# Batch 0's scores with tokens on partitions, w_spatial split in one piece, phi's reductions in one step, and new orders

## The chip, the cores and the metric

The kernel runs on one core of a Trainium2 chip. Its engines run instruction streams of their own: TensorE (PE; its weight loads are PEld), VectorE (DVE), ScalarE (ACT), GpSimd (POOL), and SyncE (SP), which here issues every DMA. The metric is the device time of one execution in microseconds (us). The kernel before takes 427.18 us, the median of three runs from 427.04 to 427.68.

## The reference

Eight batches, eight heads, 576 tokens, head size 64, 32 memories, all in fp32 (w_in and w_out arrive as float64).

```python
a = exp(phi - max(phi, axis=2)); a = a / (sum(a, axis=2) + 1e-9)   # over the 576 tokens
k_m = einsum('bhsm,bhsd->bhmd', a, k); v_m = einsum('bhsm,bhsd->bhmd', a, v)
attn = softmax(q @ k_m.T / 8)                                      # over the 32 memories
x = (attn @ v_m).transpose(0, 2, 1, 3).reshape(B, 576, 512)
h = relu(x @ w_in); u, v = h[..., :512], h[..., 512:]
v_n = (v - mean(v)) / sqrt(var(v) + 1e-6)
v_s = einsum('ts,bsd->btd', w_spatial, v_n) + b_spatial[None, :, None]
out = (u * v_s) @ w_out
```

## The kernel before

Each fp32 factor of a large product is split in a hi and a lo part, and three products of them (hi·hi, hi·lo, lo·hi) are summed in PSUM. The lo part is x − hi; it comes either from a subtraction on VectorE, or from a matmul of hi with `minus` (the negative identity), which adds −hi to x in PSUM, and a copy on ScalarE. `ON_VECTOR` names the steps that VectorE takes; the others fall to ScalarE and GpSimd, or to TensorE for a lo part.

The attention is never formed. `products` multiplies the 32 memories of each head with w_in (`mp`, split to `mh`, `ml`), and `gate` and `units` multiply the softmaxed scores (`ah`, `al`) with that. `pu` is a tile of the units (`u`), `pv` a tile of the gated branch v, which is normalised (`rs` and `sh` on GpSimd, `vr` on ScalarE) and split to `vh`, `vl`; its last 64 tokens go to `t1`, `t2`. `ps` is the product with w_spatial's transpose (`wth`, `wtl`; the last 64 tokens and the bias in `ws1`, `ws2`), `g` = u·ps is split to `gh`, `gl`, and `po` is the product with w_out (`woh`, `wol`), copied to `o` and sent out.

Each function is a generator; its yields cut it into steps, and a step is a letter with an index: P memory_weights (phi, its maximum by two transposes `mt` and `mb`, its exponentials and their sum `es`), K memories (k and v, `kvm`, the sum over tokens into the spare columns of `kvm` by a matmul with `ones`, `den`, and the transposes `tk`, `tv` that become `kT`, `vT`), Q queries (`qT`), S scores (`sc`, `sm`, then `ah`, `al`), M products, V gate, U units, G spatial, O project; and for the weights D load_win, E and L decode_win (columns 512 to 1023, which `gate` uses, and 0 to 511, which `units` uses), X prepare_out, W load_spatial, T transpose_spatial (with a `minus` matmul for the lo parts, `wt`), B prepare_bias. The decode turns float64 words to fp32 by shifts and masks (L187, L193), joins (L210, L218) and a product (L223 on VectorE, L226 on GpSimd).

A dash after a letter is one batch ahead. `START` is the order of the steps of batch 0 with all weights and the beginning of batch 1; `PLAN` is the order that every later batch repeats. Each engine executes its instructions in this written order, so an instruction that waits holds everything behind it on its engine, DMA issues on SP too. PSUM gives four single banks (`ps1`: mt, mb, kvm, tk, tv, tq, sc, mp, pv, po) and two double ones (`ps2`: wt, pu, ps), taken in turn; the first use of a bank waits for the last reader of its tile before.

## Time and profile before

| | before |
|---|---|
| median of three runs | 427.18 us (427.04 to 427.68) |
| the profiled execution: its own time, its span | 425.99 us, 424.2 us |
| PE busy in the span | 393.2 us (93%) |
| DVE, ACT, POOL busy | 299.8, 236.0, 78.9 us |
| first `pu` matmul (L663) starts | 49.23 us |
| last `po` matmul (L741) starts | 419.24 us |

The span runs from the first to the last event that the profile records; the execution's own time is 1.8 us longer. A matmul's start is exact to the record, its end is modelled, so in a row of back-to-back matmuls the distance of starts is the cost.

### The profile page before, as it was taken

How to read it: one execution, taken by the hardware profiler on the slowest of the kernel's cores; microseconds unless marked ns; L12 is line 12 of the kernel's file. 1: busy time of each engine (PE TensorE's matmuls, PEld its weight loads, DVE VectorE, ACT ScalarE, POOL GpSimd, SP SyncE). 2: the span in 40 equal slices, each digit the busy share in tenths (PEclk: the TensorE clock that was granted, in tenths of full speed). 3: DMA queues.
4: the chain of work that ended last, by engine and by line, in shares of the span. 5: the costliest groups of instructions: out<-in, count | busy, mean ns of one | idle time of the engine just before them, and what ended most of it. 6: DMA issues, size and time to landing. Idle time of an engine off the chain costs nothing.

```text
span 424.2 us, 9280 instructions
## 1 busy us (share of the span) xinstructions
PE 393.2 (93%) x3828; PEld 331.6 (78%) x3828; DVE 299.8 (71%) x560; ACT 236.0 (56%) x446; POOL 78.9 (19%) x154
## 2 busy tenths in 40 slices
PE   0295998999999999999999999999999999999995
PEld 0172786968988897978888897979798888889884
DVE  1899998995999458955897568946996568834420
ACT  1677787737753376346743575436734476248321
POOL 1345056621200022022200121002100120003100
PEclk9999899999999999999999999999999999999999
DMA  7989935507840948073922659063914500020003
GB/s 287 377 320 289 169 133 181 87 26 132 216 122 16 162 161 181 2 90 109 215 79 55 126 171 168 1 131 109 195 59 69 113 2 2 2 99 2 0 26 99
DMA packets 85790, 50.69 MB, mean 119 GB/s; under 512 B 66226, under 2 KB 70322, under 8 KB 85748
## 3 DMA queue, kind: packets, MB, share of 16 engines
q1 hardware_dynamic: 85748, 50.10, 47.9%
q8 instruction: 30, 0.49, 0.5%
q14 instruction: 12, 0.10, 0.1%
HBM read 40.65 MB, written 9.44 MB: 118 GB/s over the span
## 4 chain that ended last, share of the span: by engine, by line
PE 75%; DVE 13%; DMA 5%; ACT 4%; issue 1%; POOL 1%; SPq 0%; POOLq 0%; DVEq 0%; ACTq 0%
PE ps L701 24%; PE po L741 20%; PE pu L663 11%; PE pv L597 9%; DMA raw<-in_moe_w_in_dram 4%; PE kvm L375 4%; PE mp L565 3%; PE sc L492 2%; DVE power L210 1%; DVE win_sb L218 1%; DVE gl L725 1%; DMA out_dram<-o 1%; DVE st L621 1%; DVE sm L512 1%; PE pv L607 1%
## 5 line engine op out<-in xcount | busy, mean ns | idle before, releaser
L701 PE MATMUL ps<-wth,vh 128*128 128x288 f32 x256 | 57.0, 304 | 0.7 <-ACT u L672 0.4
L626 POOL TENSOR_SCALAR rs<-mv 128x1 f32<-128x1 f32 (+1 forms) x40 | 9.6, 241 | 249.8 <-DVE mv L623 247.2
L723 ACT CAST gh<-g 128x512 fp32r<-128x512 f32 x32 | 19.8, 620 | 63.8 <-DVE g L712 63.8
L701 PE MATMUL ps<-wth,vl 128*128 128x288 f32 x256 | 55.0, 296 | 0.0
L701 PE MATMUL ps<-wtl,vh 128*128 128x288 f32 x256 | 54.5, 294 | 0.0
L741 PE MATMUL po<-woh,gl 128*128 128x512 f32 x128 | 50.9, 398 | 0.8 <-DVE gl L725 0.8
L741 PE MATMUL po<-woh,gh 128*128 128x512 f32 x128 | 50.5, 395 | 0.0
L701 PEld LDWEIGHTS ps<-wth,vh 128*128 128x128 f32 x256 | 41.0, 188 | 12.1 <-ACT mh L574 5.0
L741 PE MATMUL po<-wol,gh 128*128 128x512 f32 x128 | 50.3, 393 | 0.0
L747 ACT COPY o<-po 128x512 f32<-128x512 f32 x36 | 20.9, 586 | 44.1 <-PE po L741 27.5
L701 PEld LDWEIGHTS ps<-wth,vl 128*128 128x128 f32 x256 | 41.0, 188 | 0.3 <-DVE vl L641 0.3
L701 PEld LDWEIGHTS ps<-wtl,vh 128*128 128x128 f32 x256 | 41.0, 188 | 0.0
L636 ACT ACTIVATE vr<-vr,sh,rs 128x512 f32<-128x512 f32 (+1 forms) x40 | 32.6, 814 | 10.2 <-POOL sh L631 9.9
L621 DVE BATCH_NORM_STATS2 st<-vr 128x6 f32<-128x512 f32 (+1 forms) x40 | 27.4, 686 | 12.1 <-ACT vr L602 11.6
L712 DVE TENSOR_TENSOR g<-u,ps 128x576 f32<-128x576 f32 x32 | 23.4, 751 | 12.5 <-PE ps L701 12.5
L741 PEld LDWEIGHTS po<-woh,gl 128*128 128x128 f32 x128 | 24.0, 188 | 8.2 <-DVE gl L725 2.8
L544 DVE TENSOR_TENSOR al<-aT,ah 128x576 fp32r<-128x576 f32 x16 | 12.1, 754 | 24.5 <-ACT ah L542 24.5
L663 PE MATMUL pu<-ah,mh 128*128 128x288 f32 x128 | 28.6, 305 | 0.0
L741 PEld LDWEIGHTS po<-wol,gh 128*128 128x128 f32 x128 | 24.0, 188 | 4.8
L741 PEld LDWEIGHTS po<-woh,gh 128*128 128x128 f32 x128 | 24.1, 188 | 4.6
L663 PE MATMUL pu<-ah,ml 128*128 128x288 f32 x128 | 27.3, 294 | 0.0
L663 PE MATMUL pu<-al,mh 128*128 128x288 f32 x128 | 27.2, 293 | 0.0
(158 smaller groups left out, 893.2 us busy)
## 6 DMA issues: line engine op xcount, KB each, us to landing
kv_sb<-in_k_dram SPq DMA_DIRECT2D x8, 1152.0 KB, 8.1
kv_sb<-in_v_dram SPq DMA_DIRECT2D x8, 1152.0 KB, 9.6
out_dram<-o SPq DMA_DIRECT2D x32, 256.0 KB, 2.4
q_sb<-in_q_dram SPq DMA_DIRECT2D x28, 288.0 KB, 6.2
phi_sb<-in_phi_dram SPq DMA_DIRECT2D x8, 576.0 KB, 4.0
raw<-in_moe_w_in_dram SPq DMA_DIRECT2D x8, 512.0 KB, 7.9
raw_out<-in_moe_w_out_dram SPq DMA_DIRECT2D x4, 512.0 KB, 5.4
w_sb<-in_moe_w_spatial_dram SPq DMA_DIRECT2D x1, 1152.0 KB, 10.8
```

What stands on the lines that cost most here:

```text
L375: nc.tensor.matmul(kvm[r][32 * j : 32 * j + 32], phi_sb[halves[r], j, i, :], kv_sb[halves[r], j, :, i * D : (i + 1) * D], start=(i == 0), ...
L544: nc.vector.tensor_tensor(al[:, r], aT[:, r], ah[:, r, 0:S].bitcast(F32), op=ALU.subtract)
L565: nc.tensor.matmul(mps[r][32 * j : 32 * j + 32, :], vT[D * r : D * r + D, 32 * j : 32 * j + 32], win_sb[D * r : D * r + D, j, cs], start=True,
L597: nc.tensor.matmul(pv, x[:, r, cs], m[:, r, DM:DFF], start=(n == 0), stop=(n == 5))
L621: nc.vector.bn_stats(st6, vr)
L636: nc.scalar.activation(vr, vr, AF.Identity, bias=sh, scale=rs)
L663: nc.tensor.matmul(pu[:, hf, 0:HALF], m[:, r, cs], a[:, r, hf * HALF : (hf + 1) * HALF], start=(n == 0), stop=(n == 5),)
L701: nc.tensor.matmul(ps[:, hf, 0:HALF], a, w[:, hf * HALF : (hf + 1) * HALF], start=(n == 0), stop=(n == len(ops) - 1),)
L712: nc.vector.tensor_tensor(g.rearrange("p (a s) -> p a s", a=2), u[:, dt, :].rearrange("p (a s) -> p a s", a=2), ps[:, :, 0:HALF], op=ALU.mult,
L723: nc.scalar.copy(hi, x)
L741: nc.tensor.matmul(po, a, w, start=(n == 0), stop=(n == 11))
L747: nc.scalar.copy(o, po)
```

## The change

1. `START` and `PLAN` are written anew, and `ON_VECTOR` names other lo parts.
2. `load_spatial` makes no copies of the last 64 columns of w_spatial. `transpose_spatial` writes its 576 columns side by side over the two banks of a double tile, takes hi by one cast and lo by one step (two `minus` matmuls where TensorE makes it); the last 64 columns come twice by two matmuls of 64 rows. The bias is cast on GpSimd.
3. `over_rows` on VectorE is one strided reduce where four steps halved the rows; on GpSimd (`es` of batches 0 and 4) the four steps stay.
4. The sum over tokens (`esm`) takes two matmuls of 128 columns where eight of 32 stood.
5. Batch 0's `scores` are `scores_by_token`: the queries are the stationary operand, so the scores stand with tokens on partitions (`sct`), the maximum and the subtraction read PSUM, and after the softmax nine TensorE transposes (`ta`) turn the result, from which `ah` and `al` are taken in PSUM. The other batches keep their way; `softmax` is their shared code, and the VectorE transposes of batch 0 go.

```diff
 ON_VECTOR = set(
...
-    E0.add E0.mul L0.add L1.add L1.mul wtl10 wtl1512 wtl40 X0.add X1.add X1.mul X1.wol es1 ml110
-    ml111 ml100 ml101 es2 es3 es5 es6 es7
+    E0.add E0.mul L0.add L1.add L1.mul X0.add X1.add X1.mul X1.wol es1 es2 es3 es5 es6 es7 ml100
+    ml101 ml110 ml111 wtl1 wtl4
...
-        for c in range(2):
-            nc.scalar.copy(w_dup[:, :, c, :], w_sb[:, :, SM:S])
-            yield
-            nc.scalar.copy(w_rem_dup[:, c, :], w_rem[:, SM:S])
-            yield
...
+        hi, lo, n = (wth[:, si], wtl[:, si], P) if si < NI else (ws1, ws2[0:SR], SR)
+        nc.scalar.copy(hi, tp)
+        yield
+        tensor = tensor_unless(f"wtl{si}")
+        if tensor:
+            for cs in (slice(0, SM // 2), slice(SM // 2, S)):
+                tensor.matmul(
+                    tp[0:n, cs],
+                    minus[0:n, 0:n],
+                    hi[0:n, cs],
...
     def over_rows(eng, to, op):
 
+        if eng is nc.vector:
+            eng.tensor_reduce(to, phi_sb.rearrange("p j i m -> p j m i"), axis=AX.X, op=op)
+            yield
+            return
...
+        for r in range(2):
+            nc.tensor.matmul(
+                esm[r],
+                es[halves[r]].rearrange("p j m -> p (j m)"),
+                ones[halves[r]],
...
+    def scores_by_token(b):
...
+        for u in range(2):
+            for r in range(2):
+                for j in range(NJ):
+                    for c in range(2):
+                        rows = slice(D * c, D * c + D)
+                        at = ((2 * u + r) * NJ + j) * MEM
+                        nc.tensor.matmul(
+                            scs[c][:, at : at + MEM],
+                            qT[rows, 2 * j + r, u * P : (u + 1) * P],
+                            kT[rows, r, 32 * j : 32 * j + 32],
...
+        for x, at in parts:
+            nc.vector.tensor_reduce(rmx[:, at], x, axis=AX.X, op=ALU.max)
+            yield
+        for x, at in parts:
+            n = at.stop - at.start
+            nc.vector.tensor_tensor(
+                smf[:, at],
+                x,
+                rmx[:, at, None].to_broadcast([P, n, MEM]),
+                op=ALU.subtract,
+            )
+            yield
+        yield from softmax(smf)
...
+        for r in range(2):
+            turned = bank(f"ta_{r}")
+            for u in range(2):
+                for c in range(2):
+                    nc.tensor.transpose(
+                        turned.rearrange("p (u n c s) -> p u c n s", u=2, n=2, c=2)[:, u, c],
+                        sm[:, 4 * c + 2 * u + r],
+                        ident,
+                    )
+            yield
...
+                nc.scalar.copy(hi[:, at], x)
+                yield
+                nc.vector.tensor_tensor(lo[:, at], x, hi[:, at].bitcast(F32), op=ALU.subtract)
+                yield
+            nc.vector.tensor_copy(ah[:, r, S:], al[:, r, SM:S].bitcast(F32))
+            yield
```

Of the orders, three places. SP's DMA issues at the start of the program, before (one row stands for all equal issues in a row; each of the eight raw pieces of w_in is 512 KB, phi is 576 KB, k, v, q and w_sb are 1152 KB each):

```order
L330 DMA phi_sb<-in_phi_dram 128x4x288
L178 DMA raw<-in_moe_w_in_dram 128x1024 x4
L260 DMA w_sb<-in_moe_w_spatial_dram 128x4x576
L261 DMA w_rem<-in_moe_w_spatial_dram 64x576
L263 DMA b_sb<-in_moe_b_spatial_dram 1x576 x2
L178 DMA raw<-in_moe_w_in_dram 128x1024 x2
L363 DMA kv_sb<-in_k_dram 128x4x576
L363 DMA kv_sb<-in_v_dram 128x4x576
L434 DMA q_all<-in_q_dram 128x4x576
L178 DMA raw<-in_moe_w_in_dram 128x1024 x2
```

and in the changed program:

```order
L334 DMA phi_sb<-in_phi_dram 128x4x288
L177 DMA raw<-in_moe_w_in_dram 128x1024 x4
L367 DMA kv_sb<-in_k_dram 128x4x576
L437 DMA q_all<-in_q_dram 128x4x576
L367 DMA kv_sb<-in_v_dram 128x4x576
L177 DMA raw<-in_moe_w_in_dram 128x1024 x4
L237 DMA raw_out<-in_moe_w_out_dram 128x1024
L259 DMA w_sb<-in_moe_w_spatial_dram 128x4x576
L260 DMA w_rem<-in_moe_w_spatial_dram 64x576
L262 DMA b_sb<-in_moe_b_spatial_dram 1x576 x2
L334 DMA phi_sb<-in_phi_dram 128x4x288
```

k, q and v now come ahead of half of w_in, and w_spatial (w_sb, w_rem) has gone from second place to behind w_in and the first piece of w_out.

TensorE's instructions up to the first `pu` and behind it, before (`mp_1_1` is the product with columns 512 to 1023 for odd heads; the rows of `kvm` with `es` are the last of batch 1's memories):

```order
L387 MATMUL kvm_0_487<-ones,es 32x2
L387 MATMUL kvm_1_488<-ones,es 32x2
L387 MATMUL kvm_0_487<-ones,es 32x2
L387 MATMUL kvm_1_488<-ones,es 32x2
L159 MATMUL wt_445<-wth,minus 128x64
L159 MATMUL mp_1_1_463<-mh,minus 128x512
L663 MATMUL pu_1_589<-ah,mh 128x288 x2
L663 MATMUL pu_1_589<-al,mh 128x288 x2
L663 MATMUL pu_1_589<-ah,ml 128x288 x2
L663 MATMUL pu_0_599<-ah,mh 128x288 x2
```

and in the changed program (`mp_1` is the half of the products that the units do not read, `mb` belongs to batch 1's phi; ahead of these rows stand the transposes `ta` of batch 0's softmaxed scores):

```order
L644 MATMUL mp_1_1_470<-win_sb,vT 32x512
L644 MATMUL mp_1_0_469<-win_sb,vT 32x512
L644 MATMUL mp_1_1_470<-win_sb,vT 32x512
L742 MATMUL pu_0_481<-ah,mh 128x288 x2
L742 MATMUL pu_0_481<-al,mh 128x288 x2
L742 MATMUL pu_0_481<-ah,ml 128x288 x2
L158 MATMUL mp_1_0_469<-mh,minus 128x512
L351 MATMUL mb_496<-ident,cmb 128x128
```

Batch 1's `kvm` matmuls and two `minus` matmuls (the first for `mp_1_0`, the second eight rows on, for `mp_1_1`) no longer stand ahead of the first `pu`; they come behind it.

GpSimd's instructions around batch 4's sum of exponentials, before:

```order
L626 TENSOR_SCALAR rs<-mv 128x1
L627 TENSOR_TENSOR rs<-rs,half_neg 128x1
L631 TENSOR_SCALAR sh<-mv,rs 128x1
L319 TENSOR_TENSOR half<-phi_sb 128x512
L321 TENSOR_TENSOR half<-half 128x4x64
L323 TENSOR_TENSOR es<-half 128x128
L325 TENSOR_TENSOR es<-es,phi_sb 128x128
L626 TENSOR_SCALAR rs<-mv 128x1
L627 TENSOR_TENSOR rs<-rs,half_neg 128x1
L631 TENSOR_SCALAR sh<-mv,rs 128x1
```

and in the changed program:

```order
L705 TENSOR_SCALAR rs<-mv 128x1
L706 TENSOR_TENSOR rs<-rs,half_neg 128x1
L710 TENSOR_SCALAR sh<-mv,rs 128x1
L323 TENSOR_TENSOR half<-phi_sb 128x512
L325 TENSOR_TENSOR half<-half 128x4x64
L705 TENSOR_SCALAR rs<-mv 128x1
L706 TENSOR_TENSOR rs<-rs,half_neg 128x1
L710 TENSOR_SCALAR sh<-mv,rs 128x1
L327 TENSOR_TENSOR es<-half 128x128
L329 TENSOR_TENSOR es<-es,phi_sb 128x128
```

The three small steps of a branch norm now stand between the second and the third of the four steps of `es`. On TensorE the transpose `mb` of the same batch's phi stands later: before, a long row of ps, po and pv matmuls lies between it and the k and v matmuls, now 34 matmuls of 512 columns (`po_1`, `pv_0`, `pv_1`, `pv_4`, `pv_2`) and 12 of 288 (`pu_2`).

## Rows read from the trace of the kernel before

**Rows 1.** The page's first part: busy time of TensorE's matmuls (PE) over the whole span, its share, and the number of instructions.
```profile
PE 393.2 (93%) x3828; PEld 331.6 (78%) x3828; DVE 299.8 (71%) x560; ACT 236.0 (56%) x446; POOL 78.9 (19%) x154
```

**Rows 2.** The span cut into stretches: from:to in us, length, busy us (and instructions) of PE, of the weight loads (PEld), VectorE (DVE), ScalarE (ACT) and GpSimd (POOL), then the granted TensorE clock (1.00 is 2.4 GHz), the DMA share and GB/s.
```profile
45.00:49.20 4.20, 4.20 (x163) 3.73 (x164) 4.06 (x12) 2.34 (x7) 0.00 (x0) 0.70 1.30 185
49.20:60.00 10.80, 10.80 (x65) 9.65 (x64) 10.33 (x24) 10.04 (x20) 4.72 (x7) 1.00 0.69 181
60.00:97.00 37.00, 34.47 (x249) 27.83 (x247) 34.58 (x61) 22.85 (x43) 16.94 (x17) 1.00 0.36 91
97.00:200.00 103.00, 102.98 (x1143) 88.51 (x1144) 73.76 (x147) 58.27 (x110) 15.64 (x40) 1.00 0.55 116
200.00:400.00 200.00, 199.46 (x1824) 171.47 (x1823) 139.72 (x268) 110.25 (x207) 25.16 (x69) 1.00 0.38 87
```

**Rows 3.** TensorE's timeline from the end of its last long idle time before the first `pu` to that: start us, duration us, engine, line, operation, out<-in, shape, count, and in brackets the idle time before with what ended it.
```profile
42.46 0.49 PE L159 MATMUL wt<-wth,minus 128*128 128x512 f32 x1 [2.59 <-ACT wth L298]
...
45.70 3.11 PE L375 MATMUL kvm<-kv_sb,phi_sb 64*32 64x128 f32 x144
48.55 0.30 PE L387 MATMUL kvm<-ones,es 64*32 64x2 f32 x16
48.78 0.30 PE L159 MATMUL wt<-wth,minus 128*128 128x64 f32 x1
48.91 0.48 PE L159 MATMUL mp<-mh,minus 128*128 128x512 f32 x1
49.23 0.43 PE L663 MATMUL pu<-ah,mh 128*128 128x288 f32 x2
```

**Rows 4.** VectorE's timeline before the first `pu`, same columns: phi's maximum (first and last of four steps), the decode's kinds of step, the wait for the last piece of w_in, and batch 0's subtraction, sum, product and first `al`.
```profile
4.78 0.69 DVE L319 TENSOR_TENSOR half<-phi_sb 128x512 f32<-128x512 f32 x1 [4.78 <-DMA phi_sb<-in_phi_dram]
...
6.29 0.29 DVE L325 TENSOR_TENSOR mx<-mx,phi_sb 128x128 f32<-128x128 f32 x1
...
11.90 1.29 DVE L193 TENSOR_SCALAR win_sb<-raw 128x1024 int32<-128x1024 int32 x2
...
14.37 1.22 DVE L210 SCALAR_TENSOR_TENSOR power<-raw,power 128x1024 int32<-128x1024 int32 x1
...
25.15 2.29 DVE L218 SCALAR_TENSOR_TENSOR win_sb<-win_sb,raw 128x1024 f32<-128x1024 f32 x1
...
28.87 0.69 DVE L187 TENSOR_SCALAR power<-raw 128x1024 int32<-128x1024 int32 x1 [0.50 <-DMA raw<-in_moe_w_in_dram]
...
38.34 2.40 DVE L512 TENSOR_TENSOR sm<-sm,rmx 128x1152 f32<-128x1152 f32 x1
...
41.97 1.35 DVE L517 TENSOR_REDUCE rsum<-sm 128x36 f32<-128x1152 f32 x1
...
43.98 1.36 DVE L522 TENSOR_TENSOR sm<-sm,rsum 128x1152 f32<-128x1152 f32 x1
...
48.16 0.75 DVE L544 TENSOR_TENSOR al<-aT,ah 128x576 fp32r<-128x576 f32 x1
```

**Rows 5.** GpSimd's timeline: one product of a decode before the first `pu`; then the four steps of batch 4's sum of exponentials (first and last), and the first and last of the three small steps of one branch norm.
```profile
38.24 3.64 POOL L226 TENSOR_TENSOR win_sb<-win_sb,power 128x512 f32<-128x512 f32 x2
...
185.86 1.29 POOL L319 TENSOR_TENSOR half<-phi_sb 128x512 f32<-128x512 f32 x1 [22.92 <-ACT phi_sb L356]
...
188.60 0.46 POOL L325 TENSOR_TENSOR es<-es,phi_sb 128x128 f32<-128x128 f32 x1
...
194.38 0.22 POOL L626 TENSOR_SCALAR rs<-mv 128x1 f32<-128x1 f32 x1 [5.32 <-DVE mv L623]
...
195.35 0.27 POOL L631 TENSOR_SCALAR sh<-mv,rs 128x1 f32<-128x1 f32 x1
```

**Rows 6.** TensorE's timeline, two kinds of matmul before the first `pu`: batch 0's k and v with the exponentials (144 matmuls in 72 pairs), and four transposes of w_spatial.
```profile
23.95 3.73 PE L375 MATMUL kvm<-kv_sb,phi_sb 64*32 64x128 f32 x144
...
39.08 0.60 PE L287 MATMUL wt<-ident,w_sb 128*128 128x128 f32 x4
```

**Rows 7.** TensorE's timeline, the instructions after its longer idle times behind the first `pu`.
```profile
73.36 0.79 PE L701 MATMUL ps<-ws,t 128*128 128x288 f32 x4 [1.08 <-DVE t L649]
...
89.97 0.50 PE L741 MATMUL po<-woh,gl 128*128 128x512 f32 x1 [0.85 <-DVE gl L725]
...
97.02 0.50 PE L597 MATMUL pv<-mh,al 128*128 128x512 f32 x1 [0.20 <-DVE al L544]
...
395.21 0.53 PE L701 MATMUL ps<-wth,vh 128*128 128x288 f32 x2 [0.31 <-ACT vh L639]
```

**Rows 8.** Batch 4's memories in the steady part, timelines of TensorE and ScalarE: the transpose `mb` of phi's maximum, the k and v matmuls, the copy of kT, and the scores that read it.
```profile
175.93 0.27 PE L347 MATMUL mb<-ident,cmb 128*128 128x128 f32 x1
...
196.13 2.25 PE L375 MATMUL kvm<-kv_sb,phi_sb 64*32 64x128 f32 x144
...
205.58 0.37 ACT L424 COPY kT<-tk 128x256 f32<-128x256 f32 x1
...
206.62 1.20 PE L492 MATMUL sc<-qT,kT 64*32 64x288 f32 x32
```

**Rows 9.** The end of the span, all engines' timeline: the last two matmuls of the last `po`, and the second of the two output DMAs.
```profile
419.00 0.39 PE L741 MATMUL po<-wol,grh 128*128 128x512 f32 x1
...
419.24 0.39 PE L741 MATMUL po<-woh,grl 128*128 128x512 f32 x1
...
420.84 0.59 SPq L753 DMA_DIRECT2D out_dram<-o  x1
```

More of the change, by code (lines that the diff above doesn't have):

```diff
@@ L453, in queries @@
                 cs = slice(j * P, (j + 1) * P)
-                nc.tensor.transpose(tq[:, cs], q_sb[:, j, 7 * D :], ident)
                 nc.tensor.transpose(tq[0:D, cs], q_sb[:, j, 8 * D :], ident)
             yield
-            for c in range(2):
-                rows = slice(D * c, D * c + D)
-                nc.scalar.copy(
-                    qT[rows, :, 256:],
-                    tq[rows].rearrange("p (h s) -> p h s", s=64)[:, :, 32 * c : 32 * c + 32],
-                )
-                yield
+            q8 = state["q8"] = one.tile([P, DM], F32, tag="t1", name="q8")
+            nc.scalar.copy(q8[0:D], tq[0:D])
+            yield
             return
@@ L484, in scores, with softmax @@
+    def softmax(smf):
+        bc = [P, 2 * NB, MEM]
+        nc.scalar.activation(smf, smf, AF.Exp, scale=SCALE)
+        yield
+        rsum = one.tile([P, 2 * NB], F32, name="rsum")
+        nc.vector.tensor_reduce(rsum, smf, axis=AX.X, op=ALU.add)
+        yield
+        nc.vector.tensor_scalar_add(rsum, rsum, 1e-9)
+        nc.vector.reciprocal(rsum, rsum)
+        yield
+        nc.vector.tensor_tensor(smf, smf, rsum[:, :, None].to_broadcast(bc), op=ALU.mult)
+        yield
     def scores(b, _):
+        if b == 0:
+            yield from scores_by_token(b)
+            return
@@ L513, in scores @@
         yield
-        nc.scalar.activation(smf, smf, AF.Exp, scale=SCALE)
-        yield
-        rsum = one.tile([P, 2 * NB], F32, name="rsum")
-        nc.vector.tensor_reduce(rsum, smf, axis=AX.X, op=ALU.add)
-        yield
-        nc.vector.tensor_scalar_add(rsum, rsum, 1e-9)
-        nc.vector.reciprocal(rsum, rsum)
-        yield
-        nc.vector.tensor_tensor(smf, smf, rsum[:, :, None].to_broadcast(bc), op=ALU.mult)
-        yield
+        yield from softmax(smf)
         aT = one.tile([P, 2, S], F32, tag="qT", name="aT")
@@ L530, in scores @@
             for c in range(2):
[L531 to L540 removed]
+                nc.vector.transpose(
+                    aT[:, r].rearrange("p (i c x) -> p c i x", c=2, x=32)[:, c], sm[:, r, c]
+                )
                 yield
```

147 lines of the change are left out of this document (83 added, 64 removed).

## The prediction

> **What bounds the kernel now.** I began with the page's busy times: TensorE computes 93% of the span [rows 1], so the question is only where the other 7% lie. The table of stretches answers it [rows 2]. From 97 to 400 us TensorE is idle 0.02 + 0.54 us in all; there nothing that another engine saves can shorten the span, and only a new wait can lengthen it. From 60 to 97 us it misses 2.53 us while VectorE is busy 34.58 of 37.00: VectorE is the bound of that stretch. Ahead of that lies the start-up: the first `pu`, with which the steady work begins, starts at 49.23 us [rows 3]. So the gain can come from three places: the first `pu`, the 2.53 us, and the tail. TensorE's timeline shows what stands right ahead of that `pu` [rows 3]: an idle time of 2.59 us, and then from 45.70 to 49.23 batch 1's k and v matmuls, their token sums and two `minus`, in a stretch whose granted clock is 0.70 on the mean [rows 2].
>
> All sums below are of the profiled execution (425.99 us, span 424.2); its difference to the median, 1.2 us, I add at the end by taking gains from 427.18.
>
> **First `pu`.** I walk the changed order with the durations of before.
>
> *DMAs.* Phi's 0.59 MB had landed at 4.78 us; the last piece of w_in, the 9.67th MB of the old order, at 28.87 [rows 4]. That is 2.65 us per MB. In the new order v is the 6.23rd MB: 4.78 + 5.64 × 2.65 = 19.7 us. The last piece of w_in is the 8.33rd: 25.3 us. w_spatial ends with the 10.18th: 30.2 us.
>
> *VectorE* has by then little else and waits for w_in. From 25.3 it does, ahead of the scores' maximum, a shift and a mask (half of the 1.29 for two, 0.65 each), a join of 1.22, then a join of the other kind and another of 1.22, and two half-width steps for w_out (half of 0.65 each): 5.6 us, so 30.9 [rows 4]. By then the scores must be there. Batch 0's k and v matmuls run from 19.9 to 23.6 by their 3.73 [rows 6]; `kT` is there some 3 us later, at 26.5, for it takes den, a scaling, a transpose and a copy.
>
> *The 32 score matmuls* have no like in the trace: 64 rows of 128 stationary columns, 32 moving. The nearest row by operands is the 144 k and v matmuls, 3.73 us for 144, 0.026 each; the nearest by stationary columns are transposes, four in 0.60, 0.15 each [rows 6]. So 0.8 to 4.8 us, from 26.5 to between 27.3 and 31.3: I take 0.1 each (3.2 us, 29.7), nearer to the transposes since the load has their 128 columns. All but the upper end is hidden before 30.9. The Trainium skill ("TensorE: Matmul & The Clock Gate", LDWEIGHTS) says that a load's time goes with its columns and not its rows, 107 ns for 128; by that the 32 would take 3.4 us. No row here has this form, and the term would stay hidden.
>
> *The softmax chain.* Two maxima, two subtractions and small third pieces replace one of each: 1.35 + 0.1 and 1.36 + 0.1. Then batch 1's phi maximum, now one reduce of 1152 elements; the sum at 41.97, with add and reciprocal up to 43.98, is 2.01; a small maximum 0.29; the product 1.36 [rows 4]. The reduce over phi I price by the row of 1152 elements, 1.35 against 1.80 for the four steps (4.78 to 6.58): a gain of 0.45, and a loss if the strided read costs more. The Trainium skill ("VectorE: DVE Perf Modes", Rules for kernel authors) warns against this very form, a reduce being the slowest operation of VectorE. The rows say by element count the reduce still wins; were it twice its row, 1.35 more per reduce would fall on this chain once. Together 1.45 + 1.46 + 1.35 + 2.01 + 0.29 + 1.36 = 7.9 us.
>
> On top comes GpSimd: a product of the decode on GpSimd takes 3.64 us [rows 5], and the subtraction beside it took 2.40 instead of 1.36 [rows 4], 1.0 more. The new order has such a product beside the same chain: 30.9 + 7.9 + 1.0 = 39.8 us. ScalarE's exponential lies beside batch 1's maximum.
>
> *To `pu`.* VectorE goes on with a product of the decode (1.3) while TensorE turns the first half (0.60 for four [rows 6]) and ScalarE casts it. Then VectorE has the low part in two pieces (0.75 for 576 columns [rows 4], with a second instruction 0.9) and w_spatial's 576 columns, 0.75; this last one frees the double bank that `pu` takes. 39.8 + 1.3 + 0.9 + 0.75 + some 0.25 of hand-over = **43.0 us, 6.2 us earlier**. VectorE's transposes of before fall away. Bounds: 41.5 if GpSimd disturbs nothing and hand-overs are free; 45.0 if TensorE again runs at the lower clock after waiting for the softmax.
>
> **Work that moves behind it.** Batch 1's k and v matmuls and two `minus` of `mp_1` now lie on TensorE's path: 2.25 [rows 8] and 2 × 0.32 (48.91 to 49.23 [rows 3]): **+2.9 us**. They were paid before the first `pu` already, at the lower clock.
>
> **The stretch up to batch 1's gate.** The waits there were 1.08 for t, 0.85 for gl, 0.20 for al [rows 7], and smaller ones, 2.53 + 0.20 in all. In the new order VectorE has by my count of rows some 5 us less to do up to batch 1's `al` (aT's transposes, four-step sums, low parts of w_spatial), and TensorE wants it 3.3 us sooner (6.2 less 2.9). So VectorE gains 1.7 on it; I let three quarters of the waits go: **−1.9 us**, bounds 0 and −2.7.
>
> **Steady batches.** Most edits cost nothing here: the reduce shortens VectorE, which has slack (73.76 of 103.00 [rows 2]); the two wide token sums replace eight narrow ones behind the k and v matmuls, tenths of a us in all. But the order of `mb` costs cover. In the row of batch 4 it lay 20.2 us ahead of the k and v matmuls [rows 8]; now 34 matmuls of 512 columns at 0.24 (419.00 to 419.24 [rows 9]) and 12 of 288 at 0.13 (in proportion), 9.7 us. What has to fit is phi's subtraction, exponential and sum. On VectorE the sum is a reduce of 1.35. Batch 4's is on GpSimd, 185.86 to 189.06, 3.2 us [rows 5], and now a branch norm's three steps (194.38 to 195.62, 1.24 [rows 5]) stand in its middle, which themselves wait for the gate behind `mb`. The token sums of batch 4 wait for that, with all of TensorE behind them: **+1.5 us**, once; bounds 0 and 4.
>
> The second place is `kT`: 1.04 us passed from the copy's start to the scores that read it, 0.67 from its end [rows 8]; before the scores TensorE has 8.1 us after the k and v matmuls in either order, and in the new one ScalarE's queue gives the copy at 8.1 to 8.2 by the sum of its rows. I count **+0.3** over all batches.
>
> **The tail.** The wait of 0.31 at 395.21 [rows 7], some 0.5 with the slower restart behind it, goes: by the sum of TensorE's rows the last gate stands 7 us ahead of its use instead of 5. The last step is a `po` with one output DMA where two stood, the second at 420.84 [rows 9], 0.5 us behind the first. **−1.0 us.**
>
> **Sum:** −6.2 + 2.9 − 1.9 + 1.8 − 1.0 = −4.4 us.
>
> **The rivals.**
> (B) *All waits vanish.* The early stretch loses all 2.7 us, and batch 4's sum and `kT` come in time. For it speaks VectorE's lead; against it the short cover of `mb`. −6.2 + 2.9 − 2.7 − 1.0 = −7.0: 420.2 us.
> (C) *The first `pu` is late.* The score matmuls cost more than the transposes' price, or w_spatial's bytes, which now come last and stand on TensorE ahead of the last scores, or the lower clock hold the chain by 4 us or more. For it: the DMA rate is taken from one stretch, and w_spatial's 30.2 leaves 0.7 us. −4.4 + 4 = −0.4: 426.8 us.
> (D) *A wait per batch: slower.* ScalarE hands over `kT` late in each of seven batches. At 0.9 us each, if most of the 1.04 us that lay between copy and scores [rows 8] turns into a wait, it is 6.3 instead of 0.3: −4.4 + 6.0 = +1.6, 428.8 us. It decides from 0.7 us per batch on. For it: the new order leaves no slack in the sum of rows; against it: the order's copies can be quicker than their sum.
>
> **How the numbers follow.** The forecast has 0.50, B 0.20, C 0.16, D 0.14. The time is the forecast's, 427.18 − 4.4 = **422.8 us**; its own range, 419.5 to 425.0, takes in the first `pu` at 41.5 to 45 in part. The range of all goes from below B (with the first `pu` 1.5 earlier, 418.7) with a margin for uncounted terms, 417.5, to 428.0, short of D. A measurement can tell 0.2%, 0.85 us: faster than 426.3 holds the forecast, B and a third of C, which is about 0.77 with what the forecast loses at its edge; the same has 0.09; slower 0.14.
>
> **What would show it.** In the new profile the first `pu` stands at 43 us with the softmax's product ending near 40; batch 1's k and v matmuls follow it at full clock; the stretch up to batch 1's gate has TensorE idle under 1 us; batch 4's token sums show a wait for GpSimd; each batch's scores at most a tenth for `kT`. A first `pu` after 46 us, or waits for ScalarE that return in each batch, would make the prediction wrong.

## The result and the profile after

The changed kernel takes 429.56 us, the median of 20 runs (427.22 to 431.04), against 427.20 us of the kernel before beside it: a ratio of 1.0053, interval 1.0037 to 1.0070. It is slower by half a per cent where 4.4 us less was forecast, and outside the range. Its profiled execution took 429.08 us, its span is 427.2 us. (The ratios leave out executions far above the fastest of their own kernel: five of e16's twelve, and no others.)

The page's first line, of the changed kernel:
```profile
PE 402.5 (94%) x3794; PEld 340.8 (80%) x3794; DVE 302.1 (71%) x511; ACT 233.5 (55%) x433; POOL 78.0 (18%) x155
```
TensorE has 34 matmul records fewer than in [rows 1] and is busy 9.3 us longer in a span that grew by 3.0: it waits less and works more slowly. Its stretches (columns as in [rows 2]):
```profile
25.00:40.00 15.00, 13.95 (x124) 10.37 (x125) 12.36 (x19) 10.55 (x17) 4.99 (x4) 0.68 1.13 210
60.00:97.00 37.00, 36.64 (x317) 30.77 (x299) 34.60 (x62) 25.11 (x49) 16.61 (x21) 1.00 0.52 140
97.00:200.00 103.00, 102.80 (x1085) 87.67 (x1091) 75.70 (x132) 56.68 (x107) 16.19 (x40) 1.00 0.57 115
200.00:400.00 200.00, 198.61 (x1802) 171.08 (x1789) 141.66 (x249) 108.79 (x207) 27.73 (x70) 1.00 0.38 87
```
From 60 to 97 us the idle time is 0.36 us where [rows 2] have 2.53. From 97 to 400 it is 0.20 + 1.39 where they have 0.56. New is the first row: from 25 to 40 us the granted clock is 0.68 on the mean. It was 0.50 (1.2 GHz) from 30.4 to 40.6 us. The 4.20 us at 0.70 ahead of the first `pu` in [rows 2] are gone, and these ten stand in their place.

TensorE's timeline in that stretch, up to the first `pu`, which answers to [rows 3]:
```profile
18.36 3.68 PE L446 MATMUL tq<-ident,q_all 128*128 128x128 f32 x16 [9.65 <-DMA q_all<-in_q_dram]
21.96 3.01 PE L379 MATMUL kvm<-kv_sb,phi_sb 64*32 64x128 f32 x144
...
26.26 0.58 PE L418 MATMUL tk<-ident,kmn 128*128 128x128 f32 x2 [0.97 <-ACT kmn L405]
...
27.62 4.56 PE L496 MATMUL sct<-kT,qT 64*128 64x32 f32 x64
32.11 1.11 PE L275 MATMUL wt<-ident,w_sb 128*128 128x128 f32 x4
33.15 0.36 PE L275 MATMUL wt<-ident,w_rem 64*128 64x64 f32 x1
33.45 1.51 PE L509 MATMUL sct<-kT,q 64*64 64x32 f32 x16
...
37.00 1.96 PE L644 MATMUL mp<-win_sb,vT 64*32 64x512 f32 x16
...
42.09 2.44 PE L275 MATMUL wt<-ident,w_sb 128*64 128x128 f32 x12
...
44.89 0.66 PE L540 MATMUL ta<-ident,sm 128*128 128x128 f32 x4
...
47.14 1.77 PE L644 MATMUL mp<-win_sb,vT 64*32 64x512 f32 x16 [0.18 <-ACT ml L163]
48.84 0.54 PE L742 MATMUL pu<-ah,mh 128*128 128x288 f32 x2
```
`pu` starts at 48.84, 0.4 us earlier than before instead of 6.2. TensorE waits 0.97 us for ScalarE ahead of `tk`, and then never for long; up to 45 us it is behind with its own work (the 64 records of `sct` are the 32 matmuls, two each). VectorE in the same stretch, which answers to [rows 4]:
```profile
4.84 2.09 DVE L319 TENSOR_REDUCE mx<-phi_sb 128x128 f32<-128x1152 f32 x1 [4.84 <-DMA phi_sb<-in_phi_dram]
...
26.53 0.69 DVE L186 TENSOR_SCALAR power<-raw 128x1024 int32<-128x1024 int32 x1 [0.79 <-DMA raw<-in_moe_w_in_dram]
...
32.20 1.29 DVE L520 TENSOR_REDUCE rmx<-sct 128x16 f32<-128x512 f32 x2 [0.30 <-PE sct L496]
34.99 0.29 DVE L520 TENSOR_REDUCE rmx<-sct 128x4 f32<-128x128 f32 x1 [1.50 <-PE sct L509]
35.20 1.48 DVE L524 TENSOR_TENSOR sm<-sct,rmx 128x512 f32<-128x512 f32 x3
36.59 2.24 DVE L319 TENSOR_REDUCE mx<-phi_sb 128x128 f32<-128x1152 f32 x1
...
41.12 0.29 DVE L345 TENSOR_REDUCE cm<-mt 128x2 f32<-128x128 f32 x1 [0.92 <-PE mt L342]
...
41.95 1.36 DVE L573 TENSOR_TENSOR sm<-sm,rsum 128x1152 f32<-128x1152 f32 x1
...
46.70 1.25 DVE L558 TENSOR_TENSOR al<-ta,ah 128x512 fp32r<-128x512 f32 x2 [2.26 <-ACT ah L556]
47.85 0.74 DVE L302 TENSOR_TENSOR ws<-wt,ws 64x576 fp32r<-64x576 f32 x1
```
VectorE now waits for the scores, 0.30 and 1.50 us, and once more for TensorE at 41.12: the softmax chain hangs on TensorE. The product ends at 43.31. Only then, from 44.89, does TensorE turn its result (`ta`), ScalarE casts it, and VectorE takes the low part `al` at 46.70 and `ws` at 47.85, which frees the bank of `pu` at 48.6.

In the steady part, TensorE at batch 5's k and v matmuls with their sums over tokens, and the longest wait of that part:
```profile
246.77 2.25 PE L379 MATMUL kvm<-kv_sb,phi_sb 64*32 64x128 f32 x144
248.95 0.39 PE L390 MATMUL kvm<-ones,es 64*128 64x2 f32 x4
249.26 0.54 PE L742 MATMUL pu<-ah,mh 128*128 128x288 f32 x2
...
287.65 0.50 PE L676 MATMUL pv<-mh,ah 128*128 128x512 f32 x1 [1.19 <-ACT ah L621]
```
From the first row's start to the `pu` behind the sums are 2.49 us. ScalarE was late with that `ah` because its copy of `o` had waited 4.34 us for an output DMA. The second trace of the same program (e5) waits there 2.83 us for the DMA, and TensorE not at all; so the 1.19 us belong to this execution (429.08 us, e5's 427.82) and not to the change:
```profile
286.44 0.58 ACT L826 COPY o<-po 128x512 f32<-128x512 f32 x1 [4.34 <-DMA out_dram<-o]
```
The end of the span, which answers to [rows 9]:
```profile
423.05 0.39 PE L820 MATMUL po<-woh,gl 128*128 128x512 f32 x1
...
424.13 0.34 SPq L829 DMA_DIRECT2D out_dram<-o  x1
```
From the last matmul to the end of the span are 4.15 us; before, 4.96.

### The profile page after: what moved, and what is told of

Its sections match the earlier page's. It is cut to its first block, busy times and chain, and to the rows that moved or that the text cites. A ratio compares the mean times of both kernels' runs of the same rounds, so it can differ in the third digit from the quotient of the medians.

```text
span 427.2 us, 9138 instructions
## 1 busy us (share of the span) xinstructions
PE 402.5 (94%) x3794; PEld 340.8 (80%) x3794; DVE 302.1 (71%) x511; ACT 233.5 (55%) x433; POOL 78.0 (18%) x155
## 4 chain that ended last, share of the span: by engine, by line
PE 82%; DMA 6%; DVE 4%; ACT 3%; SPq 2%; POOL 1%; issue 1%; ACTq 0%; DVEq 0%; POOLq 0%
PE ps L780 28%; PE po L820 22%; PE pu L742 11%; PE pv L676 8%; DMA raw<-in_moe_w_in_dram 4%; PE mp L644 4%; PE kvm L379 3%; PE sc L587 2%; DMA kv_sb<-in_v_dram 2%; PE wt L275 2%; PE sct L496 1%; DMA out_dram<-o 1%; SPq L367 1%; PE pv L686 1%; PE pv L685 1%
## 5 line engine op out<-in xcount | busy, mean ns | idle before, releaser
L705 POOL TENSOR_SCALAR rs<-mv 128x1 f32<-128x1 f32 (+1 forms) x40 | 11.4, 284 | 280.8 <-DVE mv L702 229.3
L802 ACT CAST gh<-g 128x512 fp32r<-128x512 f32 x32 | 19.9, 622 | 58.4 <-DVE g L791 58.4
L820 PE MATMUL po<-woh,gh 128*128 128x512 f32 x128 | 51.4, 402 | 0.0
L820 PE MATMUL po<-woh,gl 128*128 128x512 f32 x128 | 50.4, 393 | 0.0
L720 DVE TENSOR_TENSOR vl<-vr,vh 128x512 fp32r<-128x512 f32 x32 | 21.7, 681 | 9.9 <-ACT vh L718 9.7
```

Source lines behind the costliest of these rows:

```text
L720: nc.vector.tensor_tensor(vl[:, st, :], vr, vh[:, st, :].bitcast(F32), op=ALU.subtract)
L802: nc.scalar.copy(hi, x)
L820: nc.tensor.matmul(po, a, w, start=(n == 0), stop=(n == 11))
```

## The experiments

The theories. **Clock:** TensorE runs at 1.2 GHz for ten us while batch 0's scores are on the path, and that delays the first `pu`. **Shape:** the wide token sums cost more than the eight narrow ones. **Form:** the scores by tokens are dear at any clock. **Plan:** the new steady order loses what the start-up gains. In the expectations A1 says that the clock answers TensorE's waits, A2 that it answers the light work of the score matmuls. The ratio is to the kernel before, run on the same chip. "At 1.2 GHz" is read from the granted clock of the profiled execution, in us, ahead of the first `pu`.

| run | median us (lowest to highest) | ratio to before | first `pu` | at 1.2 GHz |
|---|---|---|---|---|
| e5 the changed kernel again | 429.53 (427.38 to 430.43) | 1.0054 [1.0036, 1.0073] | 48.97 | 30.3–40.5 |
| e1 eight sums | 429.54 (428.60 to 430.84) | 1.0070 [1.0051, 1.0088] | 49.15 | 30.1–40.3 |
| e2 four steps | 429.18 (428.69 to 433.72) | 1.0071 [1.0042, 1.0100] | 50.07 | 28.3–42.0 |
| e6 old scores | 429.42 (428.66 to 430.23) | 1.0054 [1.0040, 1.0068] | 48.97 | 29.7–36.5, 46.8–53.6 |
| e7 old plan | 433.89 (433.70 to 434.34) | 1.0163 [1.0148, 1.0177] | 48.93 | 29.4–39.6 |
| e3 filled ahead of k and v | 431.11 (428.61 to 433.03) | 1.0108 [1.0074, 1.0141] | 50.84 | 28.1–31.5, 34.9–41.7 |
| e8 wait filled | 428.24 (425.16 to 430.17) | 1.0029 [1.0005, 1.0052] | 45.59 | none |
| e9 wait filled, eight sums | 426.76 (424.52 to 427.99) | 0.9993 [0.9976, 1.0009] | 47.33 | 32.1–38.9 |
| e14 e8 with eight sums | 428.70 (428.13 to 430.66) | 1.0043 [1.0028, 1.0059] | 51.54 | 32.9–49.9 |
| e12 e9, `es0` on VectorE | 428.51 (427.99 to 429.29) | 1.0043 [1.0030, 1.0056] | 49.06 | 31.6–41.8 |
| e4 scores filled, one bank | 436.06 (435.69 to 436.53) | 1.0220 [1.0203, 1.0237] | 56.78 | 27.6–48.0 |
| e11 e4 with e9 | 437.56 (435.55 to 438.68) | 1.0241 [1.0220, 1.0263] | 57.18 | 31.4–48.5 |
| e15 scores half filled, eight sums | 434.76 (429.69 to 436.04) | 1.0159 [1.0120, 1.0197] | 52.81 | 27.3–44.4 |
| e16 scores filled (seven executions) | 426.00 (425.50 to 426.45) | 0.9973 [0.9956, 0.9989] | 46.99 | none |
| e13 both filled, eight sums | 428.02 (427.27 to 429.35) | 1.0024 [1.0013, 1.0035] | 47.14 | none |
| e17 both filled | 427.78 (426.82 to 430.84) | 1.0024 [1.0003, 1.0045] | 47.44 | none |
| e18 both filled, less | 427.69 (426.78 to 428.79) | 1.0024 [1.0008, 1.0040] | 47.85 | none |
| e10 before, its wait filled | 430.82 (429.72 to 434.20) | 1.0109 [1.0077, 1.0140] | 52.49 | none |

### The parts of the change undone

**e1**, the token sums in eight narrow matmuls again:
```diff
-        for r in range(2):
-            nc.tensor.matmul(esm[r], es[halves[r]]..., ones[halves[r]], ...)
+        for j in range(NJ):
+            for r in range(2):
+                nc.tensor.matmul(esm[r][32 * j : 32 * j + 32], es[halves[r], j, :], ...)
```


> The changed kernel with the sum over tokens in eight matmuls of 32 columns again, nothing else. Theory A: the two matmuls of 128 columns between matmuls of 32 columns cost TensorE a change of tile shape; in the changed kernel's trace each batch shows 0.18 us before them and 0.15 us behind, against nothing and a little in the kernel before. Then some 0.30 us come back in each of seven batches behind the first pu, about 2.0 us in all, and the time is some 427.5. Rival: the eight short matmuls cost as much as they save, and the time stays within 0.5 us of the changed kernel.

Batch 5's sums in e1's trace of TensorE, and one row of batch 6:
```profile
247.85 2.25 PE L379 MATMUL kvm<-kv_sb,phi_sb 64*32 64x128 f32 x144
249.84 0.29 PE L391 MATMUL kvm<-ones,es 64*32 64x2 f32 x16
250.07 0.53 PE L743 MATMUL pu<-ah,mh 128*128 128x288 f32 x2
...
297.23 0.22 PE L391 MATMUL kvm<-ones,es 64*32 64x2 f32 x3 [1.44 <-issue]
```
2.22 us to `pu` instead of 2.49: the price of the shape is 0.27 us per batch, the same in each batch where no such wait and none for GpSimd stands. The total did not fall; in the profiled execution two waits of 0.87 and 1.44 us came that no semaphore explains, of which the last section speaks. The shape's cost is shown, a gain from undoing it alone is not.

**e2**, phi's reductions on VectorE in four steps again (the `tensor_reduce` gives way to the four `tensor_tensor` of before).

> The changed kernel with phi's maximum and sums on VectorE in four steps again. Theory A: the strided reduce took 2.09 to 2.24 us in the trace, four steps 1.8, so VectorE gains 0.3 to 0.4 us at each; the two on the path before the first pu move it 0.3 to 0.7 us earlier at most, steady batches gain nothing: 0 to -0.7 us. Rival: TensorE sets the path before the first pu, and nothing moves.

Nothing gained. While TensorE is at 1.2 GHz (13.7 us here), VectorE's longer reduce is hidden.

**e5**, the changed kernel once more, as a control for e6 and e7.

> The changed kernel itself, unaltered, on the same chip as the next three, so that they can be compared with it and not only with the kernel before. All theories: the ratio to the kernel before is about 1.005, with a granted clock of 0.50 over some 10 to 18 us ahead of the first pu.

**e6**, batch 0's scores and queries as before, the orders and the rest new.

> The changed kernel with batch 0's queries and scores as before (kT stationary, 288 columns moving, VectorE's transposes to and fro), in the new order: its steps stand where the like steps of the new scores stood. Theory A (TensorE's time ahead of the first pu decides, at the lower clock): the 32 wide score matmuls take 1.2 to 2.4 us where the new ones took 4.4 + 1.5, the nine transposes go, TensorE is freed of about 5 us; VectorE gets four transposes in and four out, some 4.5 us more. If the new scores on TensorE are what pushes the first pu to 48.8, it comes 1 to 4 us sooner and the time is 1 to 3 us less. Rival C (VectorE's chain decides): the first pu comes 3 to 4.5 us later.

The same time. The old scores took TensorE less (32 matmuls in 1.59 us in the kernel before), but it then waited for w_spatial:
```profile
31.33 1.12 PE L275 MATMUL wt<-ident,w_sb 128*128 128x128 f32 x4 [3.29 <-DMA w_sb<-in_moe_w_spatial_dram]
```
and behind it 1.76 us for phi's maximum, and `pu` 0.92 us for ScalarE's `ah`; the clock was low in two stretches of 6.8 us. Going back to the old form gains nothing; what the new one costs on this path by itself, e6 does not tell, since the clock fell in it too.

**e7**, the steady order (`PLAN`) of before in the changed kernel.

> The changed kernel with the table of the steady batches as before; the table up to batch 1 and all code stay new. Theory A (the loss lies ahead of the first pu and in work moved behind it): the steady batches change by less than 1 us either way, the first pu stays at 48 to 50 us. Rival D (the new table puts a wait into each batch): the time falls by 2 to 4 us.

4.4 us slower than e5 with the first `pu` at the same place: from there to the last matmul are 378.55 us instead of 372.84. "Plan" falls.

### The clock

**e3**, idle matmuls (`Z`: four of `ident` by `ident` each) ahead of batch 0's k and v:
```diff
-    ... L0*3 L1*3 K Q D1 ...
+    ... L0*3 L1*3 K Z*7 Q D1 ...
-    ... K X1 K*4 E1 K ...
+    ... K X1 K*2 Z K*2 E1 K ...
```


> The changed kernel with 28 more 128-column matmuls of the identity on TensorE while it waits for q (9 to 18 us) and 4 in the wait ahead of tk; no data changed. Theory A (TensorE's speed sets the first pu): q's transposes and the k and v matmuls then run at the higher clock from the start, kT comes some 2 us sooner, and if the idle time is also what the later fall to 0.50 (30.5 to 40.5 us) answers, that stretch goes and the first pu comes 4 to 6 us sooner, 43 to 45 us; time 424 to 426. Rival B: the fall answers the score matmuls with their short rows, not the idle time: kT is sooner, the stretch at 0.50 stays, the first pu gains 0 to 2 us. Rival C: the path to the first pu is VectorE's and ScalarE's chain, and nothing moves.

It tells nothing of the theory: the k and v matmuls still waited for a DMA till 21.29, and a wait of 3.04 us without a semaphore stood ahead of `tk`.

**e4**, each group of eight score matmuls followed by two wide idle ones, in the last scores' bank:
```diff
+        sc = bank("sct_8")
...
+                for _ in range(2):
+                    nc.tensor.matmul(sc[:, P : 2 * P], ident, ident, start=True, stop=True)
```


> The changed kernel with two 128-column matmuls of the identity behind every eight of batch 0's score matmuls (8 more in all, some 1.2 us). Rival B of the run with early filling: the clock falls because the score matmuls keep little of the array busy; then the fall goes or shrinks here, and the first pu comes up to 4 us sooner in spite of the added 1.2 us. Theory A: the fall answers the idle times before, the stretch at 0.50 stays, and the first pu comes 1 to 2 us later.

The filling itself waited for that bank, whose reader before is ScalarE's copy of the queries:
```profile
30.44 1.22 PE L505 MATMUL sct<-ident 128*128 128x128 f32 x4 [1.54 <-ACT q L459]
```
An experiment spoilt by its own wait, though telling: the clock was low from 27.6 to 48.0 us, `pu` came at 56.78 and the kernel 6.5 us later than e5. **e11** repeated this fault together with e9's filling (bank wait 2.40 us, 437.56 us).

> The run with the ten identity matmuls ahead of tk and the eight narrow token sums, and besides two identity matmuls behind every eight of batch 0's score matmuls. In the run without them the clock still fell at 32.5 us, 8 us behind the last wait of TensorE and 5 us behind the first score matmuls. Theory A2 (the score matmuls' own light work is a second cause): the fall goes here or shrinks under 3 us; against the 1.2 us that the added matmuls take, the first pu stays at 46 to 48 us. Theory A1 (waits alone): the fall stays at 7 us or more, and the first pu comes about 1.5 us later, 48 to 49.5 us; time 428.

**e8**, the wait of 0.97 us ahead of `tk` filled with idle matmuls:
```diff
-    ... K X1 K*4 E1 K ...
+    ... K X1 K*2 Z*3 K*2 E1 K ...
```


> The changed kernel with twelve 128-column matmuls of the identity in TensorE's wait between the token sums of batch 0 and tk (24.9 to 26.3 us in the changed kernel's trace), nothing else. In four traces with the new order the granted clock fell to 0.50 some 2 to 5 us after that wait. Theory A1 (the fall answers that wait): the fall goes or comes much later, and the first pu comes up to 5 us sooner, 44 to 46 us. Rival: the fall comes all the same between 28 and 31 us, the first pu stays at 48 to 50 us or comes up to 1 us later by the added work.

The stretch from 25 to 40 us and rows of TensorE in e8's profiled execution:
```profile
25.00:40.00 15.00, 13.92 (x153) 10.94 (x151) 13.41 (x22) 12.26 (x22) 5.09 (x5) 1.00 1.13 213
```
```profile
28.75 3.76 PE L496 MATMUL sct<-kT,qT 64*128 64x32 f32 x64
32.44 0.66 PE L275 MATMUL wt<-ident,w_sb 128*128 128x128 f32 x4
...
35.31 1.09 PE L644 MATMUL mp<-win_sb,vT 64*32 64x512 f32 x16
...
38.08 0.33 PE L342 MATMUL mt<-ident,mx 128*128 128x128 f32 x1 [0.58 <-DVE mx L319]
...
45.59 0.53 PE L742 MATMUL pu<-ah,mh 128*128 128x288 f32 x2
```
The same rows at the two clocks: four transposes 0.66 and 1.11 us, `mp` 1.09 and 1.96. At full clock, 16.84 us pass from the first score to `pu`; in the changed kernel's profile 21.22 (27.62 to 48.84). The difference, 4.4 us, is the price of the ten us at 1.2 GHz on this path, by one execution of each. The one here took 425.16 us, but it was the luckiest of twelve: in no other did the mean clock of the span reach 0.998. **e9** has the filling with `Z*2`, five matmuls each, and e1's sums: 426.76 us, the same as the kernel before, in none of twelve at full clock. Its trace lies between the two: 6.8 us at 1.2 GHz, and 19.8 us from the first score (27.54) to `pu`. **e14** (e8 with e1's sums) never reached it either, and **e12**, e9 with batch 0's `es` on VectorE, put a wait of 1.45 us for `vmn` ahead of `tk`.

> The changed kernel with ten identity matmuls of 128 columns in the wait ahead of tk (in two banks that are free by then, so that tk is not held back) and with the sum over tokens in eight matmuls of 32 columns. Theory A1 (a fall of the granted clock answers a stretch with little work, and costs half a microsecond for each one at 0.50): the stretch at 0.50 is shorter than the changed kernel's 10 us and the first pu comes at 43 to 46 us. With the tile shape's 0.30 us per batch back, the time is 424 to 428, under that of the run with the filling alone (428.2) by some 1.5. Rival: the filling brought its gain by chance, and the time is 427.5 to 430.

> The changed kernel with twelve identity matmuls ahead of tk in three banks (the third of which waits 0.5 us, as in the run with this filling alone) and with the sum over tokens in eight matmuls. Theory: 1.5 to 2 us under the run with this filling alone (428.2), 426.3 to 426.8, the kernel before or a little less. Rival: the narrow sums gain nothing, 428 to 428.5.

> The run with the ten identity matmuls ahead of tk and the eight narrow token sums, and besides batch 0's sum of exponentials on VectorE instead of GpSimd, where its last step waited behind a product of the decode and held TensorE for 0.7 us at 23 us. Theory A1: one wait less ahead of the score matmuls, so the clock falls later or for less time, and kT comes up to 0.7 us sooner: the first pu 0.5 to 2 us sooner than 47.3, time 425 to 426.5, below the kernel before. Rival: VectorE's decode is held 2 us by the sum, w_in's first half is later, and the time is 427 to 428.

**e16** is the clearest: the changed kernel, with two idle matmuls behind every eight scores, now in a bank that nobody is late with, and nothing else.
```diff
-            tq = bank("tq_4")
+            tq = state["spare"] = bank("tq_4")
...
+                for _ in range(2):
+                    nc.tensor.matmul(
+                        state["spare"][D:P, 0:P], ident[:, 0:D], ident, start=True, stop=True
+                    )
```


> The changed kernel with two identity matmuls behind every eight of batch 0's score matmuls, in rows of a bank that nothing else uses, and nothing else. Theory A2 (the score matmuls' light work is the cause): the clock stays at 1.00 in nearly all runs, and the first pu comes at 46 to 47 us, 2 to 3 us sooner than the changed kernel's 48.9 although TensorE does 2.4 us more; time 426.5 to 428.5, depending on the waits that the profile calls issue. Rival: the wait ahead of tk is a cause of its own, the fall stays, 8 us or more at 0.50, the first pu at 49 to 51 us, time 430 or more.

Seven of its twelve executions ran at a mean clock of 0.998 or more and took 425.50 to 426.45 us; five ran at 0.976 to 0.980 and took 432.85 to 435.39. So A2's "nearly all runs" did not come true. None of the five was traced: what brought the clock down in them, and whether it alone made them longer, is not shown. Clock and time go together in the changed kernel too, without any edit: of its 28 executions (with e5) the 13 at a mean clock of 0.986 or more have a median of 428.57 us, the other 15 one of 430.09. In the profiled execution of e16, of 426.00 us, the stretch and TensorE:
```profile
25.00:40.00 15.00, 13.26 (x141) 10.00 (x142) 11.64 (x19) 10.77 (x19) 4.31 (x4) 1.00 1.19 208
```
```profile
27.46 1.08 PE L496 MATMUL sct<-kT,qT 64*128 64x32 f32 x16
28.48 0.65 PE L504 MATMUL tq<-ident 128*64 128x128 f32 x4
29.06 1.08 PE L496 MATMUL sct<-kT,qT 64*128 64x32 f32 x16
...
34.62 0.91 PE L513 MATMUL sct<-kT,q 64*64 64x32 f32 x16
...
46.99 0.54 PE L746 MATMUL pu<-ah,mh 128*128 128x288 f32 x2
```
Each filling is 0.58 us (28.48 to 29.06), four are 2.3: useless work of 2.3 us was added to the path, and `pu` came 1.9 us earlier than in the changed kernel. **e15**, with one idle matmul instead of two and e1's sums, is worse than none: the clock fell at 27.3 us behind waits of 1.21 and 1.07, and two waits without a semaphore (1.20 and 1.70 us) came in the steady part.

> The changed kernel with one such identity matmul behind every eight score matmuls and the sum over tokens in eight narrow matmuls. If the clock stays up with half the filling: the first pu at 45 to 46.5 us and 1.7 us less in the steady batches, time 424 to 426.5, below the kernel before (427). If half is not enough: the fall comes back in part of the runs, time 426 to 429.

**e13**, **e17** and **e18** fill both the wait and the scores (e13 with e1's sums; e18 with a smaller filling of the wait than e17).

> The run with ten identity matmuls ahead of tk and eight narrow token sums, and besides two identity matmuls of 128 rows, 64 stationary and 128 moving columns behind every eight of batch 0's score matmuls, written to rows of a bank that nothing else uses, so that no wait comes in. Theory A2 (the light work of the score matmuls): the fall goes or shrinks to under 3 us from 6.5, the first pu comes at 45.5 to 47.5 us in spite of 1 us more work. Theory A1 (waits): the fall stays at 6 to 10 us, the first pu comes at 48 to 49.5 us, the time is some 1.5 us above 426.8.

> The changed kernel (wide token sums) with two identity matmuls behind every eight score matmuls and ten in the wait ahead of tk. Theory A2: the clock stays at 1.00 in every run, as with the narrow sums, and the time is 425.5 to 427 in every run, 0.1 to 0.4% under the kernel before. Rival: the clock falls in part of the runs, which then take 432 or more; or issue waits of 1 to 2 us each bring it to 428 as with the narrow sums.

> The same with eight identity matmuls in the wait ahead of tk instead of ten. Theory A2: as the run with ten, within 0.5 us, unless the two matmuls less move an issue wait. Rival: less filling lets the clock fall in part of the runs.

At a mean clock of 0.998 or more ran 34 of the 36 executions of these three; 7 of 12 with the scores alone filled (e16); 1 of 30 with the wait alone (e8, e9, e14); none of the 28 of the changed kernel. So neither filling alone holds the clock up, and both together do. Yet all three take 427.7 to 428.0 us, where e17 and e18 were expected at 425.5 to 427: their first `pu` comes at 47.1 to 47.9, only 1.0 to 1.7 us sooner than the changed kernel's. Of the 4.4 us that the clock gives back the filling thus costs some 3 on this path (an estimate from these rows), and e13's trace has waits of 1.06 and 1.66 us without a semaphore besides. No version here beats the kernel before dependably; e16 does by 0.27% when its clock stays up, and loses 1.3% or more when it does not.

**e10** does the same to the kernel before: its wait of 2.59 us in [rows 3] is filled with 16 idle matmuls behind the transposes of w_spatial's block 3.
```diff
+        if si == 3:
+            for _ in range(16):
+                nc.tensor.matmul(tp[:, 1, P : 2 * P], ident, ident, start=True, stop=True)
```


> The kernel before with 16 identity matmuls of 128 columns in TensorE's wait of 2.59 us ahead of the first pu (42.46 us), written to unused columns of the double bank that it has; nothing else. Theory A1: the stretch at 0.50 from 44 to 47.5 us that follows this wait goes or comes later, and the first pu comes up to 1.5 us sooner than 49.2; the time is 0.5 to 2 us less. Rival: the fall has nothing to do with waits; it comes all the same, and the time is that of the kernel before or longer.

The stretch that had 0.70 in [rows 2], TensorE's longest wait behind it, and the DMA queue of that time (queue, kind: packets, MB, share):
```profile
45.00:49.20 4.20, 3.71 (x155) 2.30 (x147) 3.31 (x10) 4.11 (x10) 0.00 (x0) 1.00 1.34 143
```
```profile
51.88 0.23 PE L390 MATMUL kvm<-ones,es 64*32 64x2 f32 x6 [2.31 <-issue]
```
```profile
q8 instruction: 1, 0.02, 2.0%
```
The clock stayed up in this stretch: with the wait filled, the fall behind it did not come (the mean clock of the six executions is 0.993 to 1.0, that of the kernel before on this chip 0.990 to 0.996). The time did not gain: the filling overran the wait by 1.9 us (the next `minus` at 44.34 instead of 42.46), and two waits without a semaphore came, 2.31 and 1.85 us.

## Why the prediction was wrong

**The first `pu`: forecast 43.0, measured 48.84; the miss of 5.8 us is most of the error.** The step that failed is the walk "To `pu`" with its upper bound, "45.0 if TensorE again runs at the lower clock". The walk priced every TensorE row at 2.4 GHz and took the low clock for a matter of 2 us, behind the softmax. It came earlier, while batch 0's scores were on the path, lasted ten us, and cost about 4 (4.4 by e8 against the changed kernel; 4.0 by e16, less its filling; 6.8 us at it in e9 cost 2.95). The scores also started at 27.62 instead of 26.5. The k and v matmuls stood behind q's sixteen transposes, which the walk had left out, and started at 21.96 instead of 19.9 (in e3, where the transposes ended sooner, a DMA held them till 21.29); from there to the scores were 5.7 us, forecast 6.6. At full clock, from first score to `pu`, the walk was right by accident: 16.5 us forecast, 16.84 in e8, where the product ends 0.7 us sooner than the walk has it, counted from the first score, and the steps behind it take 1.0 longer.

**"All but the upper end is hidden before 30.9" fell with it.** I priced 32 score matmuls at 0.1 us each and left out the eight of the last head and the turns of w_spatial between them. VectorE was ready at 31.9 and had the last scores at 34.99. In e8, at full clock, the 32 take 3.69 us (28.75 to 32.44), so my 3.2 and the 0.8-to-4.8 bounds held for them; what was left out adds 1.34 and 1.51 in the changed kernel. The Trainium skill's load rule ("TensorE: Matmul & The Clock Gate", LDWEIGHTS), which gave 3.4 us, comes within 10% of that row, but by luck: e8's trace has 64 loads in it, two for each matmul, of 0.19 us each, which overlap in pairs.

**The chain and the steps behind it.** From 34.99 to the product's end at 43.31 are 8.3 us. The forecast's 8.9, without the two maxima that were done by then, is 7.6: the reduce over phi took 0.9 us more, VectorE waited 0.92 for `mt`, where TensorE was late, and the 1.0 for GpSimd did not come (the subtraction took 1.48, forecast 1.46, with GpSimd's product beside it). So the product ended 3.5 us behind the forecast. Behind it I had 3.2 us; measured are 5.5. TensorE was still at w_spatial's twelve narrow pieces (`ta` only at 44.89), ScalarE cast `ws` ahead of `ah`, and so `al` began 3.4 us behind the product instead of 1.3; it took 1.25 instead of 0.9.

**The token sums, "tenths of a us in all", were the second failed step.** Fewer matmuls were not less time: 2.49 against 2.22 us per batch from the k and v matmuls to the next `pu` (e1). Over the six batches that stood behind the first `pu` before too, 6 × 0.28 is 1.7 us (0.28 against the kernel before, 2.21). By the rows, 0.19 us of it lie ahead of the sums, where the tile form changes, and 0.08 between them and `pu`. The Trainium skill ("TensorEngine Tiling (Array Packing)", Key Properties) says that a change of tiling mode drains TensorE; the 0.19 us fit that, though a wider weight load that nothing covers would look the same.

**The reduce over phi** took 2.09 to 2.29 us, not 1.35; the four steps had 1.80 (4.78 to 6.58). The gain of 0.45 was a loss of 0.3 to 0.5; the prediction had named the condition (the strided read), and the warning it weighed was right. (The row of 1.35 also reduces 32 elements at a time and this one nine; no run separates the two.) At the low clock VectorE's slack hid it, and e2 gained nothing; in e8, at full clock, TensorE waited 0.58 us for it ahead of `mt`.

**Right:** the moved work, 2.9 forecast, 2.50 + 2 × 0.23 = 2.96 measured, though by two errors that cancel: the sums were not counted in 2.25, and 0.32 for a `minus` was too much. The early stretch's waits, −1.9 forecast, −2.2 measured (60 to 97 us). The tail, −1.0 forecast: −0.8 measured behind the last matmul, and the wait at 395.21 is gone. **Too dark:** batch 4's token sums wait 0.18 us for GpSimd instead of 1.5, and `kT` is never waited for, so rival D did not happen. **Not foreseen:** the 1.19 us at 287.65, which that execution has by chance; with it the idle time from 97 to 400 us is 1.0 longer. **The chances:** the forecast, B and a third of C add up to 0.75 (0.50 + 0.20 + 0.05), not 0.77, before the loss at the edge.

The measured sum of the spans: −0.4 + 2.96 − 2.2 + 1.0 + 1.7 − 0.8 = +2.3 of the +3.0; 0.7 us are small differences that I did not trace. In the terms of the forecast: −4.4, plus 5.8 for the first `pu`, plus 1.7 for the token sums, is +3.1; the rest cancels. Rival C had the right mechanism, the lower clock among its three causes, but with the size at 4 instead of 5.8 it ends at 426.8; the rest of the way to the slower side is the token sums.

**What stays open:** what exactly the clock answers to. Filling the wait or the scores alone does not hold it up dependably, filling both does; whether a wait, the narrow form of the score matmuls or both in sum bring it down, these runs do not tell, nor why it falls in some executions of e16 and not in others.

## What to carry to other kernels

When a change brings a stretch of small matmuls forward onto the path that sets the end, price that path at the lower clock too: here the same instructions cost about 4 us more on 17. Count a matmul by the distance of starts at its tile form, changes of form included; a fourth of the instructions was slower here. Filling with idle matmuls held the clock up, but where it stood on TensorE's path it cost some 3 of the 4 us that it won; that it pays where TensorE would wait anyway was not shown (e8, with a filled wait alone, took 428.24 us against e5's 429.53, with intervals that overlap).
